# Chunk-selected attention and a soft mixture of experts on one core: another order for the last two pairs, and rows of v 80 elements apart

## The chip, the cores and the metric

The kernel runs on one core of a Trainium2 chip. The core has five engines that run their own instruction streams and meet at semaphores: TensorE (PE, matrix products), VectorE (DVE), ScalarE (ACT), GpSimd (POOL) and SyncE (SP). The metric is the time of one execution on the device in microseconds, as the median of several runs. Beside it there is one profiled execution, whose trace gives the durations used below.

## The reference

There are 4 batches of 8 heads with 768 positions and 64 channels. Each query may look at 6 of the 24 chunks of 32 keys, those with the largest upper bound on the score, and at no later key:

```python
k_min, k_max = k_chunks.min(axis=3), k_chunks.max(axis=3)
ub = np.sum(np.maximum(q * k_min, q * k_max), axis=-1)      # per query and chunk
top_chunks = np.argsort(np.where(causal, ub, -1e9), axis=-1)[..., -6:]
scores = np.where(sel & (pos[:, None] >= pos[None, :]), scale * q @ k.T, -1e9)
attn_out = softmax(scores) @ v
```

The attention's output, as 3,072 rows of 512, goes through a soft mixture of 8 experts with 4 slots each:

```python
logits = x @ phi                                            # 3072 x 32
slot_input = softmax(logits, axis=0).T @ x                  # 32 x 512
slot_out[e] = relu(slot_input[e] @ w1[e]) @ w2[e]           # 512 -> 1024 -> 512
out = softmax(logits, axis=1) @ slot_out
```

## The kernel before

Work is cut into 16 pairs: pair i holds two heads of batch i // 4. `LAST` is 15. The instruction order on every engine is the order in which the Python code calls the helpers; there is no scheduler (`tc.manual_schedule`). Loads are issued by GpSimd, which casts float32 to bfloat16 on the way; the output is stored by SyncE.

A pair goes through these steps. `load` (lines 147 to 153) brings q and k, 192 KB each, into rings of five buffers, `ring[nm][i % 5]`; places 2 and 3 of the ring are the halves of one larger tile, filled by one load for pairs 2 and 3. `load_v` (160) brings v into one of four tiles `v_t`, where each of the 12 rows of a partition holds 64 values and a 1.0 in column 64 that makes the sum of the softmax. `transposes` and `evac_T` (225, 237) turn q and k with channels on the partitions; `kmin`, `kmax`, `qsplit`, `ubound` (TensorE, line 282) and `select` (VectorE, lines 294 and 297, and one copy on GpSimd) find the chunks, and `ns_transposes` and `evac_ns` turn the selection. `scores(i, g)` (316) computes one of six groups of score blocks into a PSUM tile of two buffers, `expo` (340) takes the exponential on ScalarE (line 347) and has GpSimd zero the upper triangle of diagonal blocks (`mask`, line 357). `pv` (362) multiplies with v: 42 matmuls of 128x65 a pair (line 375), into one PSUM tile `at_ps` with a single buffer. `normalise` (380) divides by the sums on VectorE (lines 387 and 388, tile `x_sb`) and so frees `at_ps`; `x_transposes` and `evac_x` (393, 405) turn the result.

The loop from line 618 interleaves them. In round i stand the six groups of scores of pair i, the PV matmuls of pair i - 1, the selection of pair i + 1, the transposes of pair i + 2, `normalise` and `x_transposes` of pair i - 2, and the loads of k and q of pair i + 5, of v of pair i + 2 and of one or two of the 16 weight matrices (`load_w`, line 145). In rounds 6, 10 and 14 the mixture's work for a finished batch is added: `moe_bound` (one reduce on VectorE, line 443), `moe_exp` (lines 449 to 466), `moe_exp2` (the exponentials `d_sb` and `dm` on ScalarE, lines 470 and 473), `moe_scale` (GpSimd scales `si_acc`, line 477), `moe_comb2` (three exponentials into `c_pad`), `moe_dispatch` (24 matmuls, line 509, that read `d_sb`) and `moe_ct` (transposes of `c_pad`). The logits of that batch (line 420) stand at the end of the round before. The small PSUM tiles of all these steps, `x_transposes` among them, share one place with two buffers (`p_tp`), so each waits until the one before the previous is read.

Behind the loop stands the tail: the last PV matmuls, normalisations and logits, then the experts. `experts_in` uses the first eight weight matrices, `experts_out` and `shared_out` (lines 873 and 889) the next seven, and `last_expert_out` (line 899) the one that is loaded last. It is called twice, first into the tile `so_last` and then into `so_ps`; between these VectorE makes `so_part` (931) and half of `so_all` (933). From `so_all` the output is computed and stored. `hT_pad` is a zeroed tile into which the hidden layer's transposes are copied (line 850).

Of the kernel before, what the change touches and what calls it, by code (L numbers as in the profile page):

```python
# [10 lines left out]
BF16 = mybir.dt.bfloat16  # L11
# [6 lines left out]
CH = 32  # L18
NCHUNK = 24
NQT = 6  # L20
P = 128
S = 768
D = 64
# [36 lines left out]
def kernel(  # L60
# [10 lines left out]
    nc = tc.nc  # L71
# [19 lines left out]
    st = {}  # L91

    NV = 4
    v_t = [static.tile([P, 2, NQT, D + 1], BF16, name=f"v_t{i}") for i in range(NV)]
    ident = static.tile([P, P], BF16, name="ident")

    phi_sb = static.tile([P, NDG, NS], BF16, name="phi_sb")
# [32 lines left out]
    inp = l_ctx.enter_context(tc.tile_pool(name="inp", bufs=1, side="right"))  # L130
    ring = {}
    for nm in ("k", "q"):
        one = [inp.tile([P, 2, NQT * D], BF16, name=f"{nm}_in{x}") for x in range(3)]
        two = inp.tile([P, 4, NQT * D], BF16, name=nm + "_in34")
        ring[nm] = [one[0], one[1], two[:, :2], two[:, 2:], one[2], two]

    def load_w(i):

# [8 lines left out]
    def load(i, nm):  # L147

        b, j = divmod(i, NPB)
        t = ring[nm][i % 5]  # L150
        src = {"k": k, "q": q}[nm][b, 2 * j:2 * j + 2]
        nc.gpsimd.dma_start(out=t, in_=src.rearrange("h (p g) d -> p h (g d)", p=P))  # L152
        st[nm, i] = t

    def load_pair2(nm):
        src = {"k": k, "q": q}[nm][0, 4:8]
        nc.gpsimd.dma_start(out=ring[nm][5], in_=src.rearrange("h (p g) d -> p h (g d)", p=P))
        st[nm, 2], st[nm, 3] = ring[nm][2:4]

    def load_v(i):  # L160
# [179 lines left out]
    def expo(i, g, masked=True):  # L340
        pieces = (GROUPS_LAST if i == LAST else GROUPS)[g]
        w = sum(x[2] for x in pieces)
        if w == 512:
            e = ep.tile([P, 2, 512], BF16, name="e_sb", tag="e_sb")
        else:
            e = ep3.tile([P, 2, 384], BF16, name="e3_sb", tag="e3_sb")
        nc.scalar.activation(e[:, :, :w], st.pop(("scps", i, g))[:, :, :w], func=ACT.Exp, scale=scale)  # L347

        st["e", i, g] = e
        if masked:  # L350
            mask(i, g)
# [10 lines left out]
    def pv(i, ts):  # L362
        if i == LAST and ts[0] == 0:
            st["at", i] = p_tp.tile([P, 2, 3 * (D + 1)], F32, name="at_ps", tag="tp")
        elif i == LAST and ts[0] == 3:
            st["at", i] = p_sc.tile([P, 2, 512], F32, name="at_ps", tag="sc")
        elif ts[0] == 0:
            st["at", i] = p_at.tile([P, 2, 512], F32, name="at_ps", tag="at")
        at, tb = st["at", i], 3 if i == LAST and ts[0] > 2 else 0
        for t in ts:  # L370
            for h in range(2):
                o = at[:, h, (t - tb) * (D + 1):(t - tb + 1) * (D + 1)]
                for kg in range(t + 1):
                    g, c = (BLOCK_LAST if i == LAST else BLOCK)[(kg, t)]
                    nc.tensor.matmul(  # L375
                        o, lhsT=st["e", i, g][:, h, c:c + P], rhs=v_t[i % NV][:, h, kg, :],
                        start=(kg == 0), stop=(kg == t),
                    )

    def normalise(i, t0=0, t1=NQT, at=None):  # L380
        b, j = divmod(i, NPB)
        at = st.pop(("at", i)) if at is None else at
        at = at[:, :, :(t1 - t0) * (D + 1)].rearrange("p h (t d) -> p h t d", t=t1 - t0)
        if j == 0:
            st["x", b] = xp.tile([P, NQT, H, D], BF16, name="x_sb", tag="x_sb")
        inv = tp2.tile([P, 2, NQT, 1], F32, name="inv", tag="inv")[:, :, t0:t1]
        nc.vector.reciprocal(inv, at[:, :, :, D:D + 1])
        nc.vector.tensor_tensor(  # L388
            st["x", b][:, t0:t1, 2 * j:2 * j + 2, :].rearrange("p t h d -> p h t d"),
            at[:, :, :, :D], inv.broadcast_to([P, 2, t1 - t0, D]), op=ALU.mult,  # L390
        )
# [226 lines left out]
    for i in range(1, NPAIR):  # L618
        slots = have(i - 3) and (i - 3) % NPB == NPB - 1
        if i >= EARLY:  # L620
            wt = ctx.enter_context(tc.tile_pool(name=f"wt{i}", bufs=1))
            w_sb.append(wt.tile([P, NFG * Dm], BF16, name=f"w_sb{i}"))
            weights(i)
        if have(i + 5) and not slots:
            load(i + 5, "k")
            load(i + 5, "q")
        scores(i, 0)
        expo(i, 0)
        moe(moe_max, i - 3)
        scores(i, 1)  # L630
        expo(i, 1)
        if have(i + 1):
            ubound(i + 1)
        moe(moe_bound, i - 3)
        if have(i - 2):
            normalise(i - 2)
        if i == LAST:
            moe_ct_copy(B - 2)
        if have(i + 1):
            select(i + 1)  # L640
        moe(moe_comb, i - 3)
        if have(i + 2):
            transposes(i + 2, "k")
            evac_T(i + 2, "k")
        if not slots:
            if have(i + 2):
                load_v(i + 2)
            if i < EARLY:
                weights(i)
        pv(i - 1, [0, 1, 2])  # L650
        for g in (2, 3):
            scores(i, g)
            expo(i, g, not slots)
        moe(moe_exp, i - 3)
        if slots:
            mask(i, 2)
            mask(i, 3)
        if have(i + 5) and slots:
            load(i + 5, "k")
            load(i + 5, "q")  # L660
        if have(i - 2):
            x_transposes(i - 2)
        pv(i - 1, [3] if i < LAST else [3, 4])
        if have(i + 2):
            transposes(i + 2, "q")
            evac_T(i + 2, "q")
            kmin(i + 2)
        moe(moe_exp2, i - 3)
        if have(i - 2):
            evac_x(i - 2)  # L670
        if have(i + 2):
            kmax(i + 2)
        moe(moe_scale, i - 3)
        if slots:
            if have(i + 2):
                load_v(i + 2)
            if i < EARLY:
                weights(i)
        scores(i, 4)
        expo(i, 4)  # L680
        if i == LAST:
            pv(i - 1, [5])
        moe(moe_comb2, i - 3)
        scores(i, 5)
        expo(i, 5)
        if have(i + 1):
            ns_transposes(i + 1)
            evac_ns(i + 1)
        if i < LAST:
            pv(i - 1, [4])  # L690
        moe(moe_dispatch, i - 3)
        if i < LAST:
            pv(i - 1, [5])
        if have(i + 2):
            qsplit(i + 2)
        moe(moe_ct, i - 3)
        moe(moe_logits, i - 2)
        moe(moe_copy, i - 2)
        if i == LAST - 2:
            l_ctx.close()  # L700
        if i == LAST - 1:
            u_ctx.close()

    pads = ctx.enter_context(tc.tile_pool(name="pads", bufs=1))
    siT_pad = pads.tile([P, NDG, E, CH], BF16, name="siT_pad")
    hT_pad = pads.tile([P, NFG, E, CH], BF16, name="hT_pad")
    BL = B - 1
    normalise(LAST - 1)
    pv(LAST, [0, 1, 2])
# [3 lines left out]
    def pv_last(blocks, start=False, stop=False):  # L713
        for n, (t, kg) in enumerate(blocks):
            g, c = BLOCK_LAST[(kg, t)]
            for h in range(2):
                nc.tensor.matmul(
                    at_b[:, h, (t - 3) * (D + 1):(t - 2) * (D + 1)],
                    lhsT=st["e", LAST, g][:, h, c:c + P], rhs=v_t[LAST % NV][:, h, kg, :],
                    start=(start and n == 0), stop=(stop and n == len(blocks) - 1),  # L720
                )

# [35 lines left out]
    nc.gpsimd.memset(hT_pad, 0.0)  # L758
# [237 lines left out]
```

## Time and profile before

| | us |
|---|---|
| median of 3 runs | 161.57 |
| lowest, highest | 160.94, 161.60 |
| the profiled execution | 161.03 |
| its span (first to last instruction) | 159.3 |
| TensorE busy, share | 137.7, 86% |
| VectorE busy, share | 122.7, 77% |
| ScalarE busy, share | 122.1, 77% |
| GpSimd busy, share | 103.0, 65% |
| bytes written by loads, by stores | 26.25 MB, 6.29 MB |

How to read the lines below. A line of the timeline has start and duration in us, engine, line of the kernel, operation, the tile written and the tiles read with shapes, a count of merged instructions, and in brackets the idle time of the engine just before and what ended it. "PEld" is TensorE's weight load, which overlaps its matmuls. A line of the stages has a stretch of time, the busy time of every engine with its count of instructions, the granted clock of TensorE, the mean share of time in which the core's 16 DMA engines had a packet (over 1 where they had more than one), and GB/s written. "DMA to landing" is the time from an issue to the last byte. The row "DMA" of the page is the same share in 40 slices of the span, in tenths.

### The profile page before, as it was taken

How to read it: one execution, taken by the hardware profiler on the slowest of the kernel's cores; microseconds unless marked ns; L12 is line 12 of the kernel's file. 1: busy time of each engine (PE TensorE's matmuls, PEld its weight loads, DVE VectorE, ACT ScalarE, POOL GpSimd, SP SyncE). 2: the span in 40 equal slices, each digit the busy share in tenths (PEclk: the TensorE clock that was granted, in tenths of full speed). 3: DMA queues.
4: the chain of work that ended last, by engine and by line, in shares of the span. 5: the costliest groups of instructions: out<-in, count | busy, mean ns of one | idle time of the engine just before them, and what ended most of it. 6: DMA issues, size and time to landing. Idle time of an engine off the chain costs nothing.

```text
span 159.3 us, 5926 instructions
## 1 busy us (share of the span) xinstructions
PE 137.7 (86%) x2435; PEld 93.6 (59%) x2436; DVE 122.7 (77%) x436; ACT 122.1 (77%) x168; POOL 103.0 (65%) x201
## 2 busy tenths in 40 slices
PE   7796779999999998999999989999898999978400
PEld 5473446767667776767777766767667854433000
DVE  5367889999999998999999699999952751287620
ACT  3288879999999898999989889998788632076510
POOL 6979779599797679888766976759574710000000
PEclk9999999999999999999999999999999999999965
DMA  2999999999999999999999999999999999239996
GB/s 39 149 179 202 190 208 206 185 203 205 182 208 198 202 207 200 204 183 207 198 203 203 202 203 204 201 207 194 210 203 214 215 214 200 60 116 406 406 402 251
DMA packets 40571, 32.92 MB, mean 207 GB/s; under 512 B 26336, under 2 KB 34784, under 8 KB 40544
## 3 DMA queue, kind: packets, MB, share of 16 engines
q0 software_dynamic: 38384, 26.25, 110.6%
q1 hardware_dynamic: 2160, 6.29, 10.1%
q8 instruction: 19, 0.31, 0.7%
q14 instruction: 8, 0.07, 0.1%
HBM read 52.49 MB, written 6.29 MB: 369 GB/s over the span
## 4 chain that ended last, share of the span: by engine, by line
PE 48%; ACT 17%; DVE 12%; DMA 8%; issue 6%; POOL 4%; DVEq 0%; ACTq 0%; SPq 0%; POOLq 0%
ACT e_sb L347 11%; PE sc_ps L323 9%; PE at_ps L375 8%; PE sc_ps L333 6%; DMA out_dram<-o_sb 5%; PE tr_ps L231 5%; PE xT_ps L397 4%; ACT qT L240 4%; DMA q_in<-in_q_dram 3%; DVE x_sb L388 3%; PE h_ps L834 2%; PE ub_ps L282 2%; PE ub_ps L275 1%; DVE mx L294 1%; PE so_ps L873 1%
## 5 line engine op out<-in xcount | busy, mean ns | idle before, releaser
L347 ACT ACTIVATE e_sb<-sc_ps 128x1024 bf16<-128x1024 f32 (+1 forms) x96 | 83.1, 917 | 6.6 <-PE sc_ps L333 6.0
L357 POOL TENSOR_SCALAR_AFFINE_SELECT e_sb<-e_sb 128x256 bf16<-128x256 bf16 x96 | 39.8, 437 | 12.0 <-ACT e_sb L347 11.6
L323 PE MATMUL sc_ps<-qT,kT 64*128 64x384 bf16 (+3 forms) x258 | 36.8, 306 | 2.6 <-ACT e_sb L347 1.7
L333 PE MATMUL sc_ps<-nsT,smask 64*128 64x384 bf16 (+2 forms) x294 | 38.1, 284 | 0.1
L375 PE MATMUL at_ps<-v_t,e_sb 128*128 128x65 bf16 x642 | 28.4, 194 | 1.6 <-DVE x_sb L388 1.4
L375 PEld LDWEIGHTS <-e_sb 128*128 128x128 bf16 x642 | 24.5, 98 | 3.8 <-issue 2.5
L323 PEld LDWEIGHTS <-kT 64*128 64x128 bf16 x258 | 13.9, 93 | 10.7 <-issue 5.3
L294 DVE MAX8 mx<-ub_ps 128x8 f32<-128x8 f32 (+1 forms) x192 | 16.8, 162 | 4.0 <-PE ub_ps L282 3.8
L162 POOL DMA_DIRECT2D v_t<-in_v_dram x16 | 16.6, 1040 | 3.4 <-PE xT_ps L397 1.4
L249 DVE TENSOR_REDUCE mm<-kT 128x24 bf16<-128x768 bf16 x16 | 15.1, 943 | 3.1 <-ACT kT L240 3.1
L333 PEld LDWEIGHTS <-smask 64*128 64x128 bf16 x294 | 15.0, 94 | 3.8 <-issue 0.6
L240 ACT COPY kT<-tr_ps 128x768 bf16<-128x768 bf16 x16 | 12.9, 804 | 4.3 <-PE tr_ps L231 4.3
L388 DVE TENSOR_TENSOR x_sb<-at_ps,inv 128x768 bf16<-128x768 f32 (+1 forms) x17 | 15.5, 910 | 0.6
L255 DVE TENSOR_REDUCE mm<-kT 128x24 bf16<-128x768 bf16 x16 | 15.1, 943 | 0.0
L240 ACT COPY qT<-tr_ps 128x768 bf16<-128x768 bf16 x16 | 12.8, 799 | 2.8 <-PE tr_ps L231 2.8
L145 POOL DMA_DIRECT2D w_sb<-in_moe_w_dram x16 | 11.4, 714 | 1.5 <-DMA w_sb<-in_moe_w_dram 1.5
L152 POOL DMA_DIRECT2D k_in<-in_k_dram x14 | 10.2, 726 | 3.0 <-PE tr_ps L231 1.6
L152 POOL DMA_DIRECT2D q_in<-in_q_dram x14 | 10.1, 720 | 0.5 <-PE sc_ps L333 0.3
L408 DVE COPY xT_sb<-xT_ps 128x768 bf16<-128x768 bf16 (+1 forms) x15 | 8.0, 537 | 2.5 <-PE xT_ps L397 2.5
L231 PE MATMUL tr_ps<-ident,q_in 128*64 128x128 bf16 x192 | 8.4, 223 | 1.1 <-DMA q_in<-in_q_dram 0.8
L231 PE MATMUL tr_ps<-ident,k_in 128*64 128x128 bf16 x192 | 8.7, 229 | 0.2
L397 PE MATMUL xT_ps<-ident,x_sb 128*128 128x128 bf16 x96 | 8.3, 221 | 0.3 <-DVE x_sb L388 0.3
(147 smaller groups left out, 209.0 us busy)
## 6 DMA issues: line engine op xcount, KB each, us to landing
w_sb<-in_moe_w_dram POOLq DMA_DIRECT2D x16, 1024.0 KB, 15.5
out_dram<-o_sb SPq DMA_DIRECT2D x10, 512.0 KB, 4.6
v_t<-in_v_dram POOLq DMA_DIRECT2D x16, 192.0 KB, 11.6
k_in<-in_k_dram POOLq DMA_DIRECT2D x14, 192.0 KB, 10.6
q_in<-in_q_dram POOLq DMA_DIRECT2D x14, 192.0 KB, 10.9
out_dram<-o_sb SPq DMA_DIRECT2D x2, 256.0 KB, 4.1
k_in<-in_k_dram POOLq DMA_DIRECT2D x1, 384.0 KB, 7.3
q_in<-in_q_dram POOLq DMA_DIRECT2D x1, 384.0 KB, 8.4
```

The costliest lines, as they stand in the source:

```text
L152: nc.gpsimd.dma_start(out=t, in_=src.rearrange("h (p g) d -> p h (g d)", p=P))
L162: nc.gpsimd.dma_start(out=v_t[i % NV][:, :, :, :D], in_=v[b, 2 * j:2 * j + 2].rearrange("h (g p) d -> p h g d", p=P),)
L231: nc.tensor.matmul(ps[h * 64:(h + 1) * 64, g, :], lhsT=src[:, h, g * D:(g + 1) * D], rhs=ident, is_transpose=True,)
L240: nc.scalar.copy(t.rearrange("d (p g) -> d p g", g=NQT), st.pop((nm + "ps", i)).rearrange("d g p -> d p g"),)
L249: nc.vector.tensor_reduce(mm[:, 0, 0, :], kT, axis=AX.X, op=ALU.min)
L294: nc.vector.max(mx[:, a, :], ub[:, a, :max(8, 4 * t + 4)])
L323: nc.tensor.matmul(ps[:, h, c:c + w], lhsT=kT[r, kg * P:(kg + 1) * P], rhs=qT[r, qs], start=True, stop=False,)
L333: nc.tensor.matmul(ps[:, h, c + (f - t0) * P:c + (l - t0) * P], lhsT=smask[r, x, kg].rearrange("p a b -> p (a b)"), rhs=nsT[r, (f - x * NJ ...
L347: nc.scalar.activation(e[:, :, :w], st.pop(("scps", i, g))[:, :, :w], func=ACT.Exp, scale=scale)
L357: nc.gpsimd.affine_select(out=e[:, :, c:c + P], in_=e[:, :, c:c + P], compare_op=ALU.is_ge, fill=0.0, base=0, pattern=[[0, 2], [1, P]], ch ...
L375: nc.tensor.matmul(o, lhsT=st["e", i, g][:, h, c:c + P], rhs=v_t[i % NV][:, h, kg, :], start=(kg == 0), stop=(kg == t),)
L388: nc.vector.tensor_tensor(st["x", b][:, t0:t1, 2 * j:2 * j + 2, :].rearrange("p t h d -> p h t d"), at[:, :, :, :D], inv.broadcast_to([P, ...
```

## The change

The rows of v stand 80 elements (160 bytes) apart instead of 65 (130 bytes); the matmuls still read 65 of them. The rings of k and q have four buffers instead of five. `hT_pad` moves into the pool of the tail, which lies where the tiles of the loop were, and is cleared there. Rounds 14 and 15 get an order of their own.

```diff
-    v_t = [static.tile([P, 2, NQT, D + 1], BF16, name=f"v_t{i}") for i in range(NV)]
+    VP = 80
+    v_t = [static.tile([P, 2, NQT, VP], BF16, name=f"v_t{i}") for i in range(NV)]
...
-        one = [inp.tile([P, 2, NQT * D], BF16, name=f"{nm}_in{x}") for x in range(3)]
+        one = [inp.tile([P, 2, NQT * D], BF16, name=f"{nm}_in{x}") for x in range(2)]
         two = inp.tile([P, 4, NQT * D], BF16, name=nm + "_in34")
-        ring[nm] = [one[0], one[1], two[:, :2], two[:, 2:], one[2], two]
+        ring[nm] = [one[0], one[1], two[:, :2], two[:, 2:], two]
...
-        t = ring[nm][i % 5]
+        t = ring[nm][i % 4]
...
-                        o, lhsT=st["e", i, g][:, h, c:c + P], rhs=v_t[i % NV][:, h, kg, :],
+                        o, lhsT=st["e", i, g][:, h, c:c + P], rhs=v_t[i % NV][:, h, kg, :D + 1],
...
-        moe(moe_bound, i - 3)
+        if i < LAST - 1:
+            moe(moe_bound, i - 3)
         if have(i - 2):
             normalise(i - 2)
+        if i == LAST - 1:
+            moe(moe_bound, i - 3)
...
-        pv(i - 1, [0, 1, 2])
+        if i != LAST - 1:
+            pv(i - 1, [0, 1, 2])
         for g in (2, 3):
             scores(i, g)
             expo(i, g, not slots)
+            if g == 2 and i == LAST - 1:
+                pv(i - 1, [0, 1, 2])
+            if g == 2 and i == LAST:
+                x_transposes(i - 2)
...
-        if have(i - 2):
+        if have(i - 2) and i < LAST:
             x_transposes(i - 2)
-        pv(i - 1, [3] if i < LAST else [3, 4])
+        pv(i - 1, [3])
...
-        moe(moe_exp2, i - 3)
+        if i < LAST - 1:
+            moe(moe_exp2, i - 3)
...
-        moe(moe_scale, i - 3)
+        if i < LAST - 1:
+            moe(moe_scale, i - 3)
...
         scores(i, 4)
         expo(i, 4)
+        if i == LAST - 1:
+            moe(moe_exp2, i - 3)
+            moe(moe_scale, i - 3)
         if i == LAST:
-            pv(i - 1, [5])
+            pv(i - 1, [4, 5])
...
-    hT_pad = pads.tile([P, NFG, E, CH], BF16, name="hT_pad")
...
     tail = ctx.enter_context(tc.tile_pool(name="tail", bufs=1))
+    hT_pad = tail.tile([P, NFG, E, CH], BF16, name="hT_pad")
+    nc.gpsimd.memset(hT_pad, 0.0)
```

So in round 14 the 12 PV matmuls of pair 13 (rows 0 to 2) move behind the scores of group 2, the reduce of `moe_bound` behind `normalise`, and `d_sb`, `dm` and the scaling of `si_acc` behind the exponential of group 4. In round 15 the transposes of x of pair 13 move from behind group 3 to behind group 2, and the 10 PV matmuls of row 4 of pair 14 from ahead of the scores of group 4 to behind them.

More of the change, by code (lines that the diff above doesn't have):

```diff
@@ L156, in load_pair2 @@
         src = {"k": k, "q": q}[nm][0, 4:8]
-        nc.gpsimd.dma_start(out=ring[nm][5], in_=src.rearrange("h (p g) d -> p h (g d)", p=P))
+        nc.gpsimd.dma_start(out=ring[nm][4], in_=src.rearrange("h (p g) d -> p h (g d)", p=P))
         st[nm, 2], st[nm, 3] = ring[nm][2:4]
@@ L718, in pv_last @@
                     at_b[:, h, (t - 3) * (D + 1):(t - 2) * (D + 1)],
-                    lhsT=st["e", LAST, g][:, h, c:c + P], rhs=v_t[LAST % NV][:, h, kg, :],
+                    lhsT=st["e", LAST, g][:, h, c:c + P], rhs=v_t[LAST % NV][:, h, kg, :D + 1],
                     start=(start and n == 0), stop=(stop and n == len(blocks) - 1),
@@ L757 @@
     nc.gpsimd.memset(siT_pad, 0.0)
-    nc.gpsimd.memset(hT_pad, 0.0)
     i_ctx.close()
     tail = ctx.enter_context(tc.tile_pool(name="tail", bufs=1))
+    hT_pad = tail.tile([P, NFG, E, CH], BF16, name="hT_pad")
+    nc.gpsimd.memset(hT_pad, 0.0)
     m_old = m_run[(BL + 1) % 2]
```

## The prediction

> **What bounds the kernel now.** I read the page first (shares of the span, the row of DMA), then the stages one by one, then the timeline around pairs 14 and 15 and around the last expert.
>
> ```profile
> span 159.3 us, 5926 instructions
> ...
> DMA  2999999999999999999999999999999999239996
> ```
>
> ```profile
> core 0: us, PE busy (x) PEld busy (x) DVE busy (x) ACT busy (x) POOL busy (x), PEclk, DMA share, GB/s
> 4.00:10.00 6.00, 4.72 (x67) 3.10 (x66) 2.71 (x8) 3.13 (x4) 5.93 (x10) 1.00 1.13 153
> ...
> 40.00:60.00 20.00, 19.81 (x397) 14.20 (x392) 19.19 (x70) 19.03 (x25) 15.95 (x33) 1.00 1.41 199
> ...
> 121.00:131.00 10.00, 9.43 (x194) 7.32 (x190) 5.70 (x17) 5.57 (x11) 4.69 (x8) 1.00 1.06 214
> ```
>
> Two things run side by side until 139 us. One is compute. The exponentials of a middle pair (line 347) and the two copies of line 240 follow one another on ScalarE without a break:
>
> ```profile
> 66.99 3.67 ACT L347 ACTIVATE e_sb<-sc_ps 128x1024 bf16<-128x1024 f32 x4
> 70.55 0.81 ACT L240 COPY kT<-tr_ps 128x768 bf16<-128x768 bf16 x1
> 71.39 1.51 ACT L347 ACTIVATE e_sb<-sc_ps 128x768 bf16<-128x768 f32 x2
> 72.80 0.80 ACT L240 COPY qT<-tr_ps 128x768 bf16<-128x768 bf16 x1
> 73.50 1.03 ACT L347 ACTIVATE e_sb<-sc_ps 128x1024 bf16<-128x1024 f32 x1
> ```
>
> So a middle pair costs what ScalarE needs, 6.51 us (66.99 to 73.50), and faster work on TensorE there is hidden. ScalarE waits only where a batch ends, and in the last two pairs:
>
> ```profile
> 111.22 1.94 ACT L347 ACTIVATE e_sb<-sc_ps 128x1024 bf16<-128x1024 f32 x2 [0.55 <-PE sc_ps L333]
> 113.96 1.51 ACT L347 ACTIVATE e_sb<-sc_ps 128x768 bf16<-128x768 f32 x2 [0.81 <-PE sc_ps L333]
> 115.74 0.36 ACT L470 ACTIVATE d_sb<-ld 128x192 bf16<-128x192 f32 x1 [0.27 <-POOL ld L458]
> ...
> 116.13 1.00 ACT L347 ACTIVATE e_sb<-sc_ps 128x1024 bf16<-128x1024 f32 x1
> ...
> 118.87 3.35 ACT L347 ACTIVATE e_sb<-sc_ps 128x1024 bf16<-128x1024 f32 x4 [0.45 <-PE sc_ps L333]
> 122.96 1.80 ACT L347 ACTIVATE e_sb<-sc_ps 128x1024 bf16<-128x1024 f32 x2 [0.74 <-PE sc_ps L333]
> ```
>
> The other is the stream of loads. Its DMA share is over 1 in every stage from 4 to 131 us: all 16 engines always have a packet. The last weights, issued at 117.9, land 21.0 us later, and no load of v lands sooner than 9.2 us after its issue (second answer):
>
> ```profile
> L145 POOL DMA_DIRECT2D w_sb<-in_moe_w_dram x1: 765/765/765, 117.9 to 117.9; - x1
> ...
> DMA to landing us min/median/max: 21.0/21.0/21.0
> ```
>
> ```profile
> DMA to landing us min/median/max: 9.2/11.6/13.9
> ```
>
> That puts the last landing at 138.9. The matmuls that first read these weights (line 899, the expert left for the end) start at that moment:
>
> ```profile
> 138.13 0.82 PE L889 MATMUL so_ps<-w_sb,hT_pad 128*32 128x512 bf16 x12
> 138.94 0.40 PE L899 MATMUL so_last<-w_sb,hT_pad 128*32 128x256 bf16 x8
> ...
> 138.56 0.10 PEld L899 LDWEIGHTS <-hT_pad 128*32 128x32 bf16 x1
> 138.94 0.20 PEld L899 LDWEIGHTS <-hT_pad 128*32 128x32 bf16 x8 [0.29 <-issue]
> ...
> 139.00 0.48 DVE L931 TENSOR_SCALAR so_part<-so_ps,zinv 128x256 f32<-128x256 f32 x1 [2.17 <-PE so_ps L889]
> ...
> 139.60 0.48 DVE L933 SCALAR_TENSOR_TENSOR so_all<-so_last,zinv,so_part 128x256 bf16<-128x256 f32 x1
> ```
>
> ```profile
> L889 PE MATMUL so_ps<-w_sb,hT_pad 128*32 128x512 bf16 x24 | 1.5, 379 | 0.0
> ```
>
> The twelve matmuls of line 889 go in three groups of four; one takes 379 ns (the list by line and form), so the groups stand (0.82 - 0.38)/2 = 0.22 us apart and line 899 was due at 138.13 + 3 x 0.22 = 138.79. Its first weights were loaded at 138.56, and it still began 0.15 late, with the landing. At the end of the compute the two streams arrive together. Compute is ahead by a hair: so_part ends at 139.48, so_last at 139.34, and line 933 starts at 139.60 after both. If only compute gets shorter, line 933 moves up from 139.60 to just behind so_last, about 139.39, and no further: **0.2 us is all that compute alone can give**.
>
> **The change part by part.** *The order of the last two pairs* leaves the count of matmuls and exponentials alone.
>
> ```profile
> 111.43 0.28 DVE L443 TENSOR_REDUCE mb<-pmT_ps 32x1 f32<-32x128 f32 x1
> ...
> 111.88 0.96 DVE L388 TENSOR_TENSOR x_sb<-at_ps,inv 128x768 bf16<-128x768 f32 x1
> ...
> 112.89 0.54 PE L375 MATMUL at_ps<-v_t,e_sb 128*128 128x65 bf16 x12 [0.43 <-DVE x_sb L388]
> ...
> 113.83 0.46 DVE L297 TENSOR_TENSOR ns_t<-ub_ps,mx 128x288 bf16<-128x288 f32 x1
> ...
> 115.48 0.27 PE L333 MATMUL sc_ps<-nsT,smask 64*128 64x256 bf16 x2
> ...
> 116.51 0.75 PE L509 MATMUL si_ps<-d_sb,x_sb 128*128 128x32 bf16 x24
> ```
>
> In pair 14 the 12 PV matmuls held the scores of group 2 behind x_sb. With these scores first, group 2 is ready when ScalarE is done at 113.16 (111.22 + 1.94), and the wait of 0.81 goes; x_sb no longer stands behind the reduce of 0.28. What is late next: the scores of group 4, which ended at 115.75. They follow the transposes of x, and those need the PSUM buffer that the selection (line 297) frees at 114.29, now perhaps 0.2 sooner. So the exponential of group 4 starts near 115.5, not at 116.13. Behind it (1.00) now stand d_sb, dm and the exponentials of c_pad, and TensorE has the dispatch (line 509) queued behind d_sb: that ends at 115.5 + 1.0 + 0.36 = 116.9 instead of 116.10, the dispatch starts 0.4 late, and the PV matmuls and c_pad transposes behind it bring the scores of pair 15 about 0.15 late. GpSimd scales si_acc behind two more selects, so the sum on VectorE and the x_sb behind it slip by some 0.4, which the exponentials of pair 15 cover (3.35 from 118.87); without them it would be 0.4 more. So pair 14's 0.81 is spent, and 0.15 with it.
>
> ```profile
> 121.65 0.73 PE L375 MATMUL at_ps<-v_t,e_sb 128*128 128x65 bf16 x18
> ```
>
> In pair 15 the transposes of x move into a gap before group 3, and 10 of these 18 PV matmuls behind the scores of group 4, which then start when the exponential of group 2 is done: the wait of 0.74 goes. Sum: 0.74 - 0.15, of which the last x_sb, which needs all of PV, takes over **0.4**. Bounds: -0.2 (the late d_sb alone) to 1.5 (both waits gone).
>
> *Rows of v 80 apart* start every row on a multiple of 32 bytes, where 65 (130 bytes) starts most on an odd pair. Two readers are touched. TensorE:
>
> ```profile
> 109.18 0.86 PE L375 MATMUL at_ps<-v_t,e_sb 128*128 128x65 bf16 x22
> ...
> 109.88 0.75 PE L420 MATMUL lg_ps<-phi_sb,xT_sb 128*128 128x32 bf16 x24
> ```
>
> A PV matmul takes 0.86/22 = 39 ns of such a stretch; one with weights of the same size and 32 columns 0.75/24 = 31. No aligned row is seen, so I take the middle, 4 ns less: x 42 matmuls 0.16 us a pair, bounds 0 and 0.33. Where ScalarE never waits it is hidden; at the three ends of a batch like that at 111.22 it counts: 0.5 in all. The Trainium skill ("SBUF — State Buffer", under "Door 1: The DMA port swizzle") says that each access which crosses into a new 16-byte line pays; a row of 130 bytes off a line's start crosses one more. No row here isolates it.
>
> The stream of loads is the other. By the shapes and the stages: 16.8 MB of weights at 214 GB/s (121 to 131, weights alone) take 78.4 us; 6.3 MB of k and q at 153 (4 to 10, k and q alone) 41.1; of the 134.9 us from 4.0 to 138.9 that leaves 15.4 for the 3.15 MB of v, or 204 GB/s. At the weights' rate v would take 14.7. So rows that start well can give **0.7 us** by these rows, and 12 if k and q lost nothing (29.4 at 214). The first rests on rates measured alone; of it I take 0.3, about half, since size and number of the packets stay. No row shows rows further apart; below nothing I bound it by the span, under C.
>
> *Four buffers for k and q* make a load wait for the transposes of the pair whose buffer it takes. The tightest is the load of pair 6, which would now go where pair 2 was:
>
> ```profile
> 18.59 0.53 PE L231 MATMUL tr_ps<-ident,q_in 128*64 128x128 bf16 x12
> ...
> 22.04 0.70 POOL L152 DMA_DIRECT2D k_in<-in_k_dram  x1 [0.69 <-PE ub_ps L282]
> ```
>
> Pair 2 is read until 19.12, and the load is issued at 22.04: nothing, with 2.9 us of cover. Were that gone, the selects behind it on GpSimd would be late; the stream has 9 us of work.
>
> ```profile
> 126.07 1.80 POOL L758 MEMSET hT_pad<- 128x2048 bf16 x1
> ...
> 134.17 0.29 DVE L850 COPY hT_pad<-hT_ps 128x64 bf16<-128x64 bf16 x2 [2.47 <-PE hT_ps L846]
> ```
>
> *hT_pad*, now in a pool over old tiles, is cleared once TensorE has left these, and first written 6.3 us after the clearing ended: nothing.
>
> **Sum.** Compute reaches the last expert 0.4 + 0.5 = 0.9 us earlier, the weights 0.3. The later one decides: 0.2 + 0.3 = 0.5. The profiled execution's own time was 161.03 (span 159.3 and 1.7 around it): 160.5. The median shown, 161.57, is 0.54 above it; from there it is 161.1. I predict 160.8, between.
>
> **The rivals.** *B, the stream gets out of the way.* If the writes of v's short rows set its pace, the weights land 0.7 or more earlier and compute decides: 0.9, so 160.1 from the own time. For it: each of 16 loads of v need only be 0.04 us shorter. Against it: v's 204 GB/s is already near 214. The Trainium skill ("DMA: Bandwidth & Descriptors", "How a descriptor splits into AXI transactions") counts beats of 32 bytes; 128 bytes off a beat's start touch five, on it four, which as a fifth of 15.4 us would be an estimate of 3 us. But by the same section's 256-byte blocks twelve rows from a block's start cost 83 beats at 130 bytes and 90 at 160, which speaks against the change. No run shows either.
>
> *C, slower: the stream gets longer.* A partition's twelve rows span 1,920 bytes instead of 1,560. If v's time went with that, 15.4 x 0.23 = 3.5 us; a third of it, 1.2, gives 161.03 + 1.2 - 0.2 = 162.0. It decides from 0.2 us on, since the weights are last already. Against it: no byte more is moved.
>
> *D, the order loses.* The late d_sb outlasts pair 15: compute 0.2 late, less 0.5 from PV, is 0.3 early, and without that 0.2 late: 160.8 to 161.2.
>
> *E, the rows are no faster on either side.* Then 0.4 of compute is still enough for the 0.2: 160.8.
>
> **How the numbers follow.** The forecast has 0.42, B 0.31, C 0.10, D 0.06, E 0.11. A measurement here can tell about 0.5%, 0.8 us, from no change. B sits at that edge and counts as faster unless compute falls short; of the forecast and E a little does too, where the weights gain most: 0.34 faster. Slower is C, 0.10. The rest, 0.56, is within. Range: 159.9 (B from the own time, with some more from PV) to 161.9 (D and E from the median, and half of C).
>
> **What would show it.** Right: line 899 begins with the landing and so_part is done well before it; the wait before group 4 of pair 15 gone, the exponential of pair 15's group 0 no earlier than 118.5; 22 PV matmuls in about 0.77; the last landing within 0.7 us of 138.9. Wrong: a landing before 138.2, with line 899 following line 889 without a gap (B), or after 139.2 (C); scores of pair 15 over 0.5 late.

## The result, and the profile after

| | before | after |
|---|---|---|
| median of 22 runs each, us | 161.25 | 160.64 |
| ratio, 95% interval | | 0.9952, 0.9931 to 0.9972 |
| the profiled execution, us | 161.03 | 160.31 |
| its span, us | 159.3 | 158.6 |

The changed kernel is 0.5% faster, just within what was called no change, and the time forecast, 160.8, is 0.16 above the median. The ratio leaves out one slow run of each kernel, over 1.5% above that kernel's fastest, and is not the quotient of the medians. Most of the way there was another one than forecast.

The page of the changed kernel (most lines of the kernel stand 1 to 14 further down): its span, the row of GB/s in 40 slices, and the queue of the stores with packets, MB and their share of 16 engines' time.

```profile
span 158.6 us, 5941 instructions
...
GB/s 38 154 182 203 188 207 206 185 202 205 183 206 200 203 207 196 206 185 204 202 203 204 201 205 200 201 207 197 207 204 213 217 211 209 75 82 424 418 419 247
...
q1 hardware_dynamic: 2160, 6.29, 9.8%
```

The two lines of the page before that answer to the last two:

```profile
GB/s 39 149 179 202 190 208 206 185 203 205 182 208 198 202 207 200 204 183 207 198 203 203 202 203 204 201 207 194 210 203 214 215 214 200 60 116 406 406 402 251
...
q1 hardware_dynamic: 2160, 6.29, 10.1%
```

While the loads run, the rates are alike. In the slices 37 to 39, where the output is stored, they rise from 402 to 406 GB/s to 418 to 424, for the same 2,160 packets and 6.29 MB. The stages of the changed kernel say the same (the columns are those of the stages above); the last is a stretch of stores alone, and behind it stands the same stretch of the kernel before:

```profile
4.00:10.00 6.00, 4.97 (x70) 3.21 (x70) 2.83 (x9) 3.13 (x4) 5.93 (x10) 1.00 1.15 161
40.00:60.00 20.00, 19.72 (x402) 14.36 (x400) 19.23 (x70) 18.87 (x25) 15.79 (x32) 1.00 1.41 199
121.00:131.00 10.00, 9.43 (x197) 7.17 (x200) 6.00 (x18) 5.69 (x11) 4.50 (x8) 1.00 1.07 215
143.50:155.50 12.00, 4.95 (x22) 1.63 (x22) 6.05 (x10) 5.39 (x8) 0.00 (x0) 0.87 1.03 420
```

```profile
143.50:155.50 12.00, 4.92 (x22) 1.62 (x22) 6.35 (x10) 5.39 (x8) 0.00 (x0) 0.87 1.02 406
```

The middle of the loop and the weights' rate have not moved (199 and 199, 214 and 215). The first pairs of loads came at 161 instead of 153 GB/s; other executions of kernels with rows 80 apart show 144 to 182 there, so this belongs to the execution.

ScalarE in pairs 14 and 15, in the timeline after (start, duration, engine, line, operation, tiles, count, and in brackets the wait before it):

```profile
110.94 3.43 ACT L348 ACTIVATE e_sb<-sc_ps 128x1024 bf16<-128x1024 f32 x4 [0.51 <-PE sc_ps L334]
115.23 1.02 ACT L348 ACTIVATE e_sb<-sc_ps 128x1024 bf16<-128x1024 f32 x1 [0.86 <-PE sc_ps L334]
116.15 0.35 ACT L471 ACTIVATE d_sb<-ld 128x192 bf16<-128x192 f32 x1
...
118.69 4.74 ACT L348 ACTIVATE e_sb<-sc_ps 128x1024 bf16<-128x1024 f32 x5 [0.77 <-PE sc_ps L334]
123.67 0.81 ACT L348 ACTIVATE e_sb<-sc_ps 128x768 bf16<-128x768 f32 x1 [0.25 <-PE sc_ps L334]
```

The waits ahead of group 2 of pair 14 (0.81) and group 4 of pair 15 (0.74) are gone, and others have come: 0.86 ahead of group 4 of pair 14, 0.77 instead of 0.45 at the start of pair 15, 0.25 at the last group. From group 0 of pair 14 to the end of the last exponential it is 123.67 + 0.81 - 110.94 = 13.54 us; before it was 122.96 + 1.80 - 111.22 = 13.54. The new order, as it stands, is worth nothing.

What follows d_sb in the same timeline: TensorE's dispatch, GpSimd's scaling, VectorE's sum and the x_sb behind it, and the PV matmuls and the scores of group 2 of pair 15 that stand behind x_sb:

```profile
116.55 0.75 PE L510 MATMUL si_ps<-d_sb,x_sb 128*128 128x32 bf16 x24 [0.47 <-ACT d_sb L471]
...
117.06 0.51 POOL L478 TENSOR_TENSOR si_acc<-si_acc,dm 128x160 f32<-128x160 f32 x1
...
117.61 0.29 DVE L519 TENSOR_TENSOR si_acc<-si_acc,si_ps 128x128 f32<-128x128 f32 x1 [1.43 <-POOL si_acc L478]
...
118.57 0.96 DVE L389 TENSOR_TENSOR x_sb<-at_ps,inv 128x768 bf16<-128x768 f32 x1
...
119.63 0.53 PE L376 MATMUL at_ps<-v_t,e_sb 128*128 128x65 bf16 x12 [0.55 <-PE sc_ps L334]
...
120.08 0.34 PE L324 MATMUL sc_ps<-qT,kT 64*128 64x384 bf16 x2
```

The list by line for the last weights, and for the loads of v:

```profile
L146 POOL DMA_DIRECT2D w_sb<-in_moe_w_dram x1: 765/765/765, 117.5 to 117.5; - x1
...
DMA to landing us min/median/max: 20.7/20.7/20.7
```

```profile
DMA to landing us min/median/max: 8.7/11.2/13.7
```

The last weights are issued 0.4 earlier and land 20.7 later: at 138.2 instead of 138.9. The end of the compute, again in the timeline after:

```profile
137.18 1.47 PE L903 MATMUL so_ps<-w_sb,hT_pad 128*32 128x512 bf16 x24
138.26 0.42 PEld L913 LDWEIGHTS <-hT_pad 128*32 128x32 bf16 x9
138.48 0.39 PE L913 MATMUL so_last<-w_sb,hT_pad 128*32 128x256 bf16 x8
138.71 0.48 DVE L945 TENSOR_SCALAR so_part<-so_ps,zinv 128x256 f32<-128x256 f32 x1 [2.17 <-PE so_ps L903]
139.24 0.40 PE L913 MATMUL so_ps<-w_sb,hT_pad 128*32 128x256 bf16 x8 [0.37 <-DVE so_part L945]
...
139.30 0.48 DVE L947 SCALAR_TENSOR_TENSOR so_all<-so_last,zinv,so_part 128x256 bf16<-128x256 f32 x1
```

Line 913 (899 before) follows line 903 without a wait for the weights, and line 947 starts at 139.30 instead of 139.60. Added up from the two timelines: pair 14 starts 0.28 earlier (110.94 against 111.22), the last two pairs give nothing, the first matmul that reads so_all starts 0.29 earlier (139.84 against 140.13), and from there to the end it is 158.58 - 139.84 = 18.74 us instead of 159.31 - 140.13 = 19.17 (spans to two places from the trace). Of the 0.72 us that the span lost, 0.43 went in the output stage, in which the change edits nothing.

The 0.28 was already there when the exponentials of pair 6 began; the kernel before and the changed one:

```profile
53.84 1.94 ACT L347 ACTIVATE e_sb<-sc_ps 128x1024 bf16<-128x1024 f32 x2 [0.55 <-PE sc_ps L333]
```

```profile
53.56 1.94 ACT L348 ACTIVATE e_sb<-sc_ps 128x1024 bf16<-128x1024 f32 x2 [0.51 <-PE sc_ps L334]
```

From there to pair 14 both kernels took 57.38 us (111.22 - 53.84 and 110.94 - 53.56). The very first exponential started 0.11 earlier (12.65 against 12.76).

Two rows for the rest. PV, 22 matmuls (0.86 before), and the clearing of hT_pad with its first writer:

```profile
108.93 0.83 PE L376 MATMUL at_ps<-v_t,e_sb 128*128 128x65 bf16 x22
```

```profile
125.79 1.80 POOL L774 MEMSET hT_pad<- 128x2048 bf16 x1
133.88 0.29 DVE L864 COPY hT_pad<-hT_ps 128x64 bf16<-128x64 bf16 x2 [2.47 <-PE hT_ps L860]
```

### The profile page after: what moved, and what is told of

Same layout as the page of the kernel before. It is cut to its first block, busy times and chain, and to the rows that moved or that the text cites. A ratio compares the mean times of both kernels' runs of the same rounds, so it can differ in the third digit from the quotient of the medians.

```text
span 158.6 us, 5941 instructions
## 1 busy us (share of the span) xinstructions
PE 137.4 (87%) x2436; PEld 93.3 (59%) x2436; DVE 122.5 (77%) x436; ACT 122.2 (77%) x168; POOL 102.5 (65%) x201
## 3 DMA queue, kind: packets, MB, share of 16 engines
q1 hardware_dynamic: 2160, 6.29, 9.8%
HBM read 52.49 MB, written 6.29 MB: 371 GB/s over the span
## 4 chain that ended last, share of the span: by engine, by line
PE 45%; ACT 17%; DVE 11%; DMA 8%; POOL 7%; issue 7%; DVEq 0%; ACTq 0%; SPq 0%; POOLq 0%
ACT e_sb L348 11%; PE sc_ps L324 8%; PE at_ps L376 7%; PE sc_ps L334 6%; DMA out_dram<-o_sb 5%; PE tr_ps L232 4%; PE xT_ps L398 4%; ACT qT L241 3%; DMA q_in<-in_q_dram 3%; POOL e_sb L358 3%; PE h_ps L848 2%; DVE x_sb L389 2%; PE ub_ps L283 2%; DVE mx L295 1%; PE ub_ps L276 1%
## 5 line engine op out<-in xcount | busy, mean ns | idle before, releaser
L358 POOL TENSOR_SCALAR_AFFINE_SELECT e_sb<-e_sb 128x256 bf16<-128x256 bf16 x96 | 39.3, 432 | 11.5 <-ACT e_sb L348 11.2
L376 PE MATMUL at_ps<-v_t,e_sb 128*128 128x65 bf16 x642 | 27.6, 193 | 1.8 <-DVE x_sb L389 1.0
L376 PEld LDWEIGHTS <-e_sb 128*128 128x128 bf16 x642 | 23.7, 97 | 4.4 <-issue 2.8
```

The costliest lines, as they stand in the source:

```text
L358: nc.gpsimd.affine_select(out=e[:, :, c:c + P], in_=e[:, :, c:c + P], compare_op=ALU.is_ge, fill=0.0, base=0, pattern=[[0, 2], [1, P]], ch ...
L376: nc.tensor.matmul(o, lhsT=st["e", i, g][:, h, c:c + P], rhs=v_t[i % NV][:, h, kg, :D + 1], start=(kg == 0), stop=(kg == t),)
```

## The experiments

### The parts one by one

Three kernels start from the one before. The first takes the order of rounds 14 and 15 alone; against the changed kernel it is

```diff
-    VP = 80
+    VP = D + 1
...
-        t = ring[nm][i % 4]
+        t = ring[nm][i % 5]
...
-    hT_pad = tail.tile([P, NFG, E, CH], BF16, name="hT_pad")
+    hT_pad = pads.tile([P, NFG, E, CH], BF16, name="hT_pad")
```

> The kernel before with the new order of rounds 14 and 15 alone (rows of v 65 apart, five buffers, hT_pad where it was). Theory R (the rows of v are what helps: the last weights land 0.6 us earlier, 138.3 instead of 138.9, and each PV run is shorter): the order alone moves the exponentials of pair 15 by less than 0.2 us, the weights land at 138.9 +- 0.2, the ratio is 1.000 +- 0.002. Theory O (the order takes out the 0.74 us wait of pair 15 and so makes the gain): ratio 0.995 to 0.997, the last exponential of pair 15 ends 0.3 us or more earlier than before. Theory B (both are needed, since compute and the weights end within 0.2 us of each other): ratio 0.998 to 0.999, line 899 begins with the landing.

The second takes the rows, the buffers and the place of `hT_pad`, and all of the old order; against the kernel before:

```diff
+    VP = 80
-    v_t = [static.tile([P, 2, NQT, D + 1], BF16, name=f"v_t{i}") for i in range(NV)]
+    v_t = [static.tile([P, 2, NQT, VP], BF16, name=f"v_t{i}") for i in range(NV)]
...
-        t = ring[nm][i % 5]
+        t = ring[nm][i % 4]
...
-    hT_pad = pads.tile([P, NFG, E, CH], BF16, name="hT_pad")
...
+    hT_pad = tail.tile([P, NFG, E, CH], BF16, name="hT_pad")
```

> The kernel before with rows of v 80 apart, four buffers and hT_pad in the tail, but the old order. Theory R: ratio 0.995 to 0.997, the weights land at 138.3 +- 0.2, the 22 PV matmuls of rows 4 and 5 take 0.84 us instead of 0.86, and the work of round 10 stands 0.28 us earlier as it does in the changed kernel. Theory O: ratio 1.000 +- 0.002. Theory B: ratio 0.998 to 0.999; the weights land earlier but line 903 (889 before) still begins at 137.4 or later, so that the landing isn't waited for and compute decides.

The third is the second with `VP = D + 1`: the buffers and the place of `hT_pad` only.

> The kernel before with four buffers for k and q and hT_pad in the tail alone (rows 65 apart, old order). By the prediction these two cost nothing, ratio 1.000 +- 0.002 in every theory; the landing of the last weights at 138.9 +- 0.2. A rival: the new place of the tiles in SBUF, or the loads' waits, is what moves the landing; then the weights land 0.4 us or more earlier here too, and the ratio is 0.998 or less.

| | ratio, 95% interval | weights land, us | line 942's matmul to the end, us |
|---|---|---|---|
| order alone | 0.9995, 0.9960 to 1.0031 | 139.1 | 19.16 |
| rows and buffers | 0.9959, 0.9926 to 0.9991 | 138.4 | 18.77 |
| buffers alone | 1.0003, 0.9968 to 1.0038 | 138.3 | 19.18 |

Line 942 (956 in the changed kernel) is the first product that reads so_all; with it the output stage begins. Theory R has its ratios: everything comes with the rows. But its reason does not hold. The kernel with buffers alone had its weights at 138.3 too, 0.6 before the kernel before, and gained nothing. So the landing moves by so much between executions, and the gain is not tied to it. What goes with the rows without exception is the last column. From group 0 of pair 14 to the end of the last exponential the order alone took 13.61 us and rows and buffers 13.50, against 13.54 before: there the order as it stands costs some 0.05 us and the rows give about as much.

### d_sb back

```diff
-        if i < LAST - 1:
-            moe(moe_exp2, i - 3)
+        moe(moe_exp2, i - 3)
...
-        if i < LAST - 1:
-            moe(moe_scale, i - 3)
+        moe(moe_scale, i - 3)
...
-        if i == LAST - 1:
-            moe(moe_exp2, i - 3)
-            moe(moe_scale, i - 3)
```

> The changed kernel with d_sb, dm and the scaling of round 14 back ahead of the scores of group 4. The prediction says that their new place makes the dispatch 0.4 us late and the scores of pair 15 0.15 late. If so: the wait of TensorE before the dispatch of round 14 (0.47 us in the changed kernel) is gone, the exponentials of pair 15 begin up to 0.15 us earlier, and the ratio to the kernel before is 0.001 lower than that of the changed kernel (0.994 against 0.995) where compute decides. The rival: ScalarE, which is then behind by the two exponentials (0.4 us) before group 4, only waits less; pair 15 begins at 118.7 as in the changed kernel, and the ratio is 0.995.

The ratio is 0.9932 (0.9908 to 0.9957). Its timeline, from d_sb to the last expert:

```profile
115.05 0.36 ACT L471 ACTIVATE d_sb<-ld 128x192 bf16<-128x192 f32 x1 [0.91 <-POOL ld L459]
...
115.71 0.75 PE L510 MATMUL si_ps<-d_sb,x_sb 128*128 128x32 bf16 x24
...
117.62 0.96 DVE L389 TENSOR_TENSOR x_sb<-at_ps,inv 128x768 bf16<-128x768 f32 x1
...
118.18 4.46 ACT L348 ACTIVATE e_sb<-sc_ps 128x1024 bf16<-128x1024 f32 x5 [0.45 <-PE sc_ps L334]
...
118.68 0.53 PE L376 MATMUL at_ps<-v_t,e_sb 128*128 128x65 bf16 x12
...
119.26 0.34 PE L324 MATMUL sc_ps<-qT,kT 64*128 64x384 bf16 x2
...
122.89 0.81 ACT L348 ACTIVATE e_sb<-sc_ps 128x768 bf16<-128x768 f32 x1 [0.25 <-PE sc_ps L334]
...
138.64 0.40 PE L908 MATMUL so_last<-w_sb,hT_pad 128*32 128x256 bf16 x8 [0.76 <-DMA w_sb<-in_moe_w_dram]
```

The dispatch starts at 115.71 instead of 116.55, pair 15 waits 0.45 instead of 0.77, and the stretch from group 0 of pair 14 (at 110.71) to the end of the last exponential is 122.89 + 0.81 - 110.71 = 12.99 us instead of 13.54. The mixed kernel below, which also has d_sb back, took 12.99 again. So the order is worth 0.55 us to compute against the kernel before (0.51 against rows and buffers with the old order), and the new place of d_sb, dm and the scaling took all of it back. Half of the 0.55 is pair 15's start, 7.75 us behind pair 14's instead of 7.47, where 0.15 at most was expected. The other half lies within pair 15, which takes 5.80 us from its first exponential to the end of its last instead of 5.51. By the traces x_sb is what is late there: counted from pair 14 it ends 0.72 later (119.53 against 118.58, less the 0.23 by which pair 14 began later), in both the PV matmuls start 0.10 behind it, and the scores of group 2 stand behind these on TensorE. The bracket of the PV line names the scores before it; the time fits x_sb. (One edit moved all three pieces back, so the two halves were not tested one by one.) Now the last expert waits 0.76 for its weights, which here landed at 138.6: the other stream takes most of what compute gained. This is the best kernel of the study and is faster than the one before; against the changed kernel the two intervals overlap, so a further gain is not shown.

### Where the output tiles begin

Tiles are laid out one behind the other in a partition. By the addresses of the built programs the four v tiles grow from 1,560 bytes (taking 1,568) to 1,920, so the output tiles, which lie behind them, move up by 4 x 352 = 1,408 bytes. The five output tiles `o_sb`, from which every store reads, began at byte 136,576, which is 384 past a multiple of 512; now they begin at 137,984, 256 past one. An unused tile ahead of them moves them alone:

```diff
+    pad_o = tail.tile([P, 64], BF16, name="pad_o")
     op = ctx.enter_context(tc.tile_pool(name="op", bufs=5))
```

It was put into the kernel before (tiles at 0) and into the changed one (tiles at 384 again). A third kernel, the one with d_sb back, has output buffers 4,160 bytes apart:

```diff
-        o_sb = op.tile([P, 2, Dm], F32, name="o_sb", tag="o_sb")
+        o_sb = op.tile([P, 2 * Dm + 16], F32, name="o_sb", tag="o_sb")[:, :2 * Dm].rearrange("p (x d) -> p x d", x=2)
```

> The kernel before (rows of v 65 apart, old order) with an unused tile of 128 bytes ahead of the output tiles, so that these begin at a multiple of 512 bytes of their partition instead of 384 past one; nothing else moves. Theory S (the output stage gets 0.4 us shorter in the kernels with rows 80 apart because the longer v tiles shift the output tiles from 384 to 256 past a multiple of 512): all store packets of 4096 bytes take 159 ns instead of 159 to 190, the stage from the first matmul that reads so_all to the end takes 18.8 us instead of 19.2, ratio 0.9975 +- 0.002. Theory N (the 0.4 us of the output stage is chance, or comes with the weights): 19.2 us, ratio 1.000. Beside it: if rows 65 apart are what makes the early pairs later, the exponentials of pair 6 begin at 53.8 to 54.1 as in the other three kernels with such rows.

> The changed kernel with the same unused tile of 128 bytes, which puts its output tiles 384 past a multiple of 512, as they were before the change. Theory S: store packets spread from 159 to 190 ns again, the output stage takes 19.2 us, and the ratio to the kernel before rises from 0.995 to 0.9975 +- 0.002. Theory N: 18.8 us and 0.995. If rows 80 apart are what makes the early pairs earlier, the exponentials of pair 6 begin at 53.3 to 53.6 as in the other three kernels with such rows; if that was chance, anywhere from 53.3 to 54.1.

> The changed kernel with d_sb back, its five output buffers 4160 bytes apart, so that they begin 256, 320, 384, 448 and 0 past a multiple of 512. It prices the alignment by itself: if a multiple of 256 is what matters, the packets of four of the ten stores of 256 rows (those of the buffers at 0 and 256) take 159 ns and those of the other six 163 to 166 on average; if it were a multiple of 512, only those at 0 (two stores); if 384 alone is bad, all but two are at 159.

The stretch of stores in the kernel before with the tiles moved to 0:

```profile
143.50:155.50 12.00, 4.95 (x22) 1.63 (x22) 6.29 (x10) 5.39 (x8) 0.00 (x0) 0.81 1.03 419
```

and in the changed kernel with the tiles moved back to 384:

```profile
143.50:155.50 12.00, 4.64 (x18) 1.36 (x14) 5.93 (x9) 5.39 (x8) 0.00 (x0) 0.77 1.02 404
```

406 GB/s became 419, and 420 became 404. The kernel before with nothing but 128 unused bytes is 0.9962 of its time (0.9933 to 0.9992); the changed kernel with its output tiles where they used to be is 0.9996 (0.9968 to 1.0024). The first kernel has neither the rows nor the order, the second has both. Theory S holds. The mixed kernel (0.9951, 0.9913 to 0.9990, 161.4 ns on average and 18.86 us) decides nothing: six of its ten stores of 256 rows at 164.3 ns would give 162.2 on average, two of ten 160.1, and it lies between. Its stores overlap, so a packet can't be put down to one buffer; by position its buffer at 448 looked almost free, which asked for kernels with one offset each: 448 and 416 in the kernel before (64 and 32 unused bytes), 320 in the changed one.

> The kernel before with an unused tile of 64 bytes ahead of the output tiles, which puts these 448 past a multiple of 512. Theory 256 (any begin that is no multiple of 256 costs the same): store packets of 4096 bytes take 164 ns on average, as at 384, and the output stage 19.2 us. Theory 64-to-go (the last stretch of the mixed kernel's stores of that buffer looked almost free): 159 to 161 ns, 18.8 to 18.9 us. Early pairs: if rows 65 apart make them later, the exponentials of pair 6 begin at 53.7 to 54.1.

> The kernel before with an unused tile of 32 bytes ahead of the output tiles: 416 past a multiple of 512, and 32 past one of 64. Theory 256: 164 ns, 19.2 us. A rival, that 64 bytes matter too: more than 165 ns and more than 19.3 us. Early pairs as in the kernel with 448: 53.7 to 54.1 if rows 65 apart make them later.

> The changed kernel with an unused tile of 64 bytes ahead of the output tiles: 320 past a multiple of 512. Theory 256: 164 ns and 19.2 us. Rival: 163 ns or less, since the mixed kernel's stores of that buffer were at 163. Early pairs: if rows 80 apart make them earlier, the exponentials of pair 6 begin at 53.1 to 53.7; if that is chance, up to 54.1.

All kernels with one offset, by the 1,280 store packets of 4,096 bytes in each trace:

| output tiles begin, past a multiple of 512 | kernels | mean packet, ns | packets over 161 ns | output stage, us |
|---|---|---|---|---|
| 0 | 1 | 159.1 | 2% | 18.77 |
| 256 | 5 | 159.1 | 1 to 2% | 18.74 to 18.77 |
| 320 | 1 | 163.9 | 43% | 19.19 |
| 384 | 4 | 164.2 to 164.4 | 43 to 44% | 19.16 to 19.18 |
| 416 | 1 | 164.3 | 45% | 19.20 |
| 448 | 1 | 164.4 | 47% | 19.18 |

Theory 256 has all three, and the thought that 448 is nearly free falls. Whatever else a kernel had in it, its output stage followed this one address. (The kernels with 320, 416 and 448 were run once, at 160.68, 163.26 and 161.53 us; their traces are used, and not their times.)

### Rows 65 apart, everything else in place

Over these kernels the first pairs also seemed earlier with rows 80 apart. To separate the rows from the addresses, the changed kernel got its rows 65 apart inside tiles of the new size, and was run beside the changed kernel itself:

```diff
-    v_t = [static.tile([P, 2, NQT, VP], BF16, name=f"v_t{i}") for i in range(NV)]
+    VR = D + 1
+    v_t = [
+        static.tile([P, 2 * NQT * VP], BF16, name=f"v_t{i}")[:, :2 * NQT * VR].rearrange("p (h g d) -> p h g d", h=2, g=NQT)
+        for i in range(NV)
+    ]
```

> The changed kernel with the rows of v 65 apart inside tiles of the new size: every address but those of the rows themselves stays, so the output tiles remain at a multiple of 256. Theory P (aligned rows save TensorE 0.16 us a pair, which counts in the first pairs, where TensorE is busy 9.9 of 10 us): the exponentials of pair 6 begin at 53.7 to 54.3, 0.3 to 0.6 later than in the changed kernel run beside it; ratio to that 1.002 to 1.004. Theory H (the saving is hidden there, and what was seen is the spread of the first loads): 53.1 to 53.7 in both, ratio 1.000 +- 0.002. In both the store packets take 159 ns and the output stage 18.8 us, and the 22 PV matmuls of rows 4 and 5 take 0.86 us.

> The changed kernel again, for the comparison with rows 65 apart in place on the same chip: ratio to the kernel before 0.995 +- 0.002, exponentials of pair 6 from 53.1 to 53.7 by theory P and up to 54.1 if their place is chance; output stage 18.8 us in every theory.

The ratios to the kernel before are 0.9979 (0.9939 to 1.0019) and 0.9985 (0.9950 to 1.0019): they do not tell the two apart, and the changed kernel's ratio is nearer to 1 than at first (the two intervals share 0.9950 to 0.9972; by the medians, 160.57 against 161.16, it is as far below as then). The 22 PV matmuls took 0.86 us with rows 65 apart in place and 0.83 in the changed kernel again, as expected. The exponentials of pair 6, with rows 65 apart in place and in the changed kernel again:

```profile
54.56 1.02 ACT L352 ACTIVATE e_sb<-sc_ps 128x1024 bf16<-128x1024 f32 x1 [0.55 <-PE sc_ps L338]
```

```profile
53.57 1.94 ACT L348 ACTIVATE e_sb<-sc_ps 128x1024 bf16<-128x1024 f32 x2 [0.51 <-PE sc_ps L334]
```

That is 0.99 apart, and 54.56 is past the 54.3 of theory P, but by the trace the very first exponential already started at 13.35 against 12.60, before a row of v is read. The 0.75 of it belongs to the first loads; 0.24 is left. From the first exponential to those of pair 6 the seven kernels with rows 65 apart took 41.07 to 41.96 us (41.42 on average), the seven with rows 80 apart 40.63 to 41.32 (40.98); five of the latter lie below all of the former. So a gain of 0.2 to 0.4 us in the first pairs is likely, and no ratio shows it. Of these kernels the one run again also waited for its weights:

```profile
139.00 0.40 PE L913 MATMUL so_last<-w_sb,hT_pad 128*32 128x256 bf16 x8 [0.31 <-DMA w_sb<-in_moe_w_dram]
```

## Why the prediction came out

**Two streams that end together: right.** By the traces, the matmuls of the last expert began 0.04 to 0.05 us after the landing in seven of the fourteen executions, and in the other seven 0.13 to 1.5 us after it, behind the compute. With d_sb back compute was 0.55 shorter and waited 0.76. That "the later one decides" is shown. In the profiled changed kernel it was compute: line 913 did not begin with the landing, as the first sign asked, and so_part was not done well before it.

**The order, 0.74 - 0.15, of which 0.4 reach the last x_sb: wrong.** The wait ahead of group 4 of pair 15 is gone and pair 15 starts at 118.69, no earlier than 118.5, as the signs asked. What the forecast took as late came out near its sizes. Counted from pair 14 and against rows and buffers with the old order, the dispatch is 0.36 late (0.4 forecast), x_sb 0.46 ("some 0.4") and pair 15 0.09 (0.15). The step that failed is the gain within pair 15: "the wait of 0.74 goes", with the late x_sb one "which the exponentials of pair 15 cover". Pair 15 takes 5.80 us instead of 5.85, so 0.05 came of the 0.74. Some 0.29 of it went because x_sb was not covered: the scores of group 2 stand behind the PV matmuls that wait for it. Of the rest most was never there. With d_sb back too a wait of 0.25 stays ahead of the last group, whose scores now stand behind 22 PV matmuls instead of 12; in the changed kernel:

```profile
122.29 0.84 PE L376 MATMUL at_ps<-v_t,e_sb 128*128 128x65 bf16 x22
...
123.30 0.27 PE L334 MATMUL sc_ps<-nsT,smask 64*128 64x256 bf16 x2
```

Measured, the new place of d_sb, dm and the scaling costs 0.55, the whole gain of the order. Rival D named the late d_sb, with a chance of 0.06, and comes nearest to the order's worth: it put compute 0.2 late and the forecast 0.4 early, and some 0.05 late was measured.

**Rows on TensorE, 0.16 us a pair and 0.5 in all: aligned rows are faster, both sizes are off.** By the trace the next PV matmul starts 29 ns behind one with an aligned row, and mostly 32 to 33 ns before (31 to 34 on average by row), except behind rows whose offset is a multiple of 16 bytes, where it was mostly 29 too. (With aligned rows one distance in five is 35 ns, at the same places of each pair; why was not tried.) The prediction's 39 ns divide the whole stretch by 22, with the last matmul's own 0.19 us in it; from start to start it is 0.67/21 = 32. The runs of 22, 12 and 8 matmuls of a pair shrink by 34, 24 and 4 ns: 0.06 us a pair, where 0.16 was taken, and 22 matmuls take 0.83 to 0.84, not 0.77. At a batch's end the wait went from 0.55 to 0.51, yet from pair 6 to pair 14, with two such ends in it, both kernels take 57.38 us: pairs 8 and 12 took 6.58 us instead of 6.50 in all seven kernels with rows 80 apart, for a reason not looked for. So behind pair 6 no more than the 0.05 of the last two pairs is left of the 0.5. The Trainium skill ("SBUF — State Buffer", "Door 1: The DMA port swizzle") has the 16-byte lines; the trace agrees with their size and gives the price, 3 to 4 ns a matmul. But the prediction's count of them is wrong: 130 bytes touch nine such lines from a line's start and from any even offset within one, so "crosses one more" isn't the reason, and the reason stays open. That the saving is hidden elsewhere was wrong for the first pairs, if the likely 0.2 to 0.4 there is indeed from the rows.

**Rows in the stream of loads, 0.3: not shown.** The packets of v took 32.2 ns on average in both kernels, and in all fourteen traces 32.1 to 32.4. The landing at 138.2 was within the 0.7 of the forecast, but over all traces the landing ranged from 138.3 to 139.6 with rows 65 apart, and with rows 80 apart from 137.9 to 139.0. The averages, 138.8 and 138.4, differ by about what was forecast, but with seven traces each that spread over 1.1 to 1.4 us this is not shown to be the rows. B and C, the rivals on this side, both fall: rows further apart cost the stream nothing, and gave it nothing that can be told from this spread.

**Four buffers and hT_pad, nothing: right.** Alone they are 1.0003 (0.9968 to 1.0038). hT_pad is first written 6.3 us after its clearing ended (133.88 - 127.59), as before.

**What the sum left out: the output stage.** Longer tiles move every address behind them, and the prediction costed the rows only where v itself is read and written. It forecast 0.5 ahead of the output and got 0.29, then nothing in the output and got 0.43. That the number came out is luck: terms that gave next to nothing were in the sum, and one that gave most was missing. What the forecast's own terms are worth was measured in the changed kernel with its output tiles at 384: 0.9996 (0.9968 to 1.0024), where 0.5 us would be 0.9969, at the very edge of that interval. Where the rest of the 0.72 comes from stays open; the first pairs are likely, and of their 0.28 in the profiled execution 0.11 stood before a row of v was read. The Trainium skill ("DMA: Bandwidth & Descriptors", "How a descriptor splits into AXI transactions") has the rule that was weighed for v and belonged to the stores: a transaction starts at a multiple of 256 bytes, and what lies ahead of a descriptor's start is fetched for nothing. The boundary agrees with the table above. Its count of beats would make a packet of 4,096 bytes 132 instead of 128 beats at 384, an estimate of 164.1 ns (159.1 x 132/128), against 164.2 to 164.4 measured; at 320 it would be 130 beats and 161.6, and at 448 134 and 166.6, but the runs show 163.9 and 164.4. A price that grows with the offset is not seen; instead 43 to 47% of the packets take more than 161 ns, up to 198, and the rest 159.

**The time.** From the median of 161.57 over 3 runs 161.1 was worked out, from the one execution 160.5. Over 22 runs the kernel before has 161.25, and 0.5 less would be 160.75, against 160.64 measured: the middle between the two was the better start.

## What to carry to other kernels

A tile that changes its size moves all tiles allocated behind it, so look at where the tiles begin that DMA reads before crediting the edit itself: here 128 unused bytes gave 0.4% where the whole change gave 0.5%. Where two streams end together, shorten one and see who waits next; the gain of an order can be spent by small work that moved behind something else, so before calling a late tile covered, look at what stands behind its reader on the reader's engine. To attribute a change of half a per cent, undo its parts one at a time and compare stages between traces: the end of the stream of loads alone moved by 1.1 us or more between executions of kernels with the same rows.

## What the runs showed of the hardware

- Stores from SBUF whose rows of 4,096 bytes begin at a multiple of 256 take 159.1 ns a packet; at 64, 128, 160 or 192 bytes past one 163.9 to 164.4, and the stage of 6.29 MB is 0.4 us longer (19.16 to 19.20 against 18.74 to 18.77).
- The slow packets are not spread evenly: with the tiles at 384, the first 16 packets of a store of 128 (by start) average 159 to 162 ns and the last 16 some 165 to 175. Why was not tried.
- Behind a matmul of 128x65 whose moving rows start off a multiple of 16 bytes the next one mostly starts after 32 to 33 ns instead of 29; an offset of 16 past a multiple of 32 is as fast as an aligned one, and 8 past one of 16 is not.
- Cast loads of 128-byte rows into SBUF took 32.1 to 32.4 ns a packet, whether the rows lay 130 or 160 bytes apart.
